# Writing out the order of every engine beside the products of a blocked attention and gated-unit kernel

## The chip, the cores and the metric

The kernel runs on one core of a Trainium2 chip. The metric is the device time of the whole kernel in microseconds (us). TensorE (PE) multiplies matrices into PSUM, VectorE (DVE), ScalarE (ACT) and GpSimd (POOL) work element by element, and SyncE (SP) issues most DMAs. Each engine works through its own instructions in the order in which they were put out, and waits for others by semaphores.

## The reference

Eight batches of 576 positions with eight heads of 64 go through attention, and the 4608 resulting rows of 512 through a gated unit with an inner width of 1536. Four heads see the last 32 positions, four see every 32nd position.

```python
B, H, S, D = q.shape
scores = scale * np.matmul(q, k.transpose(0, 1, 3, 2))
mask_local = (rel >= 0) & (rel < stride)
mask_strided = (rel >= 0) & (pos[None, :] % stride == pos[:, None] % stride)
scores = np.where(masks[None, :, :, :], scores, -1000000000.0)
...
attn = np.exp(scores)
attn = attn / (np.sum(attn, axis=-1, keepdims=True) + 1e-09)
...
gate = 1.0 / (1.0 + np.exp(-(x @ w_gate)))
val = x @ w_val
return (gate * val @ w_out).astype(np.float32)
```

## The kernel before

**Arithmetic.** Every float32 operand of the gated unit is split into a high part, which TensorE's fp32r format holds, and the low rest. A product is three matmuls: high x high, high x low, low x high (`three`, L407 to L409; `outs`, L437 to L442). All of them are of 128 x 128 weights by 512 columns.

**Stages.** The first phase computes the attention of batches 0, 1 and 2 (512 of their 576 positions are a "chunk"; the 64 others are kept for the end), brings in the weights, and computes the gated unit of batch 0 directly. Then come four superblocks of two chunks each: batches 1 and 2, 3 and 4, 5 and 6, and in the last batch 7 and the rests of all eight. A superblock multiplies two chunks with the two matrices of the gate and the value (g and v) in 2 x 2 blocks by seven products, P1 to P7, instead of eight. It does so in 6 pairs of weight blocks, 14 products a pair (P1 of g, P1 of v, P5 of g and so on), and then has 8 groups of output products, four for each chunk. The weights' mixtures that the seven products need are formed once, in superblock 1 (`load_mix`: sums and low parts on GpSimd, high parts on ScalarE), stored in DRAM, and loaded by the later superblocks.

**Beside a pair.** TensorE accumulates into six banks, called g1, g2, g5 and v1, v2, v5. `pair_of_chunks` copies (ACT) P1, P5 and P6 out of their banks, takes sigmoids (ACT, L539), adds (DVE, L537) and multiplies (DVE, L538, into `h`). A bank can be written again when its reader is done. `load_outs` splits `h` into high and low parts (L579, L580) for the output products. `store` copies the four sums of a chunk out of PSUM, ScalarE the first and third, VectorE the second and fourth, into the buffers of `OBS` (L458), and SP sends them out (L452).

**Attention beside it.** During a superblock, the attention of the next superblock's two batches runs in four steps per batch (`pair`): score matmuls (L189), mask, maximum and subtraction (`soft`, L203 to L209), exponential (ACT, L213), sum and division (`norm`, L217 to L220), eight 32x32 block transposes on VectorE (`turn_blocks`, L242), weighing matmuls (L270), copies to `raw` (`split_high`, L301). Batches 0 to 2 use TensorE's transposes (L228) and ScalarE's copies (L250) in place of VectorE's. When the eight steps are done, `mix_input` forms the seven mixtures of the next chunks (T: subtractions on VectorE, L342; h: high parts on ScalarE, L352; l: low parts on VectorE, L354).

**What sets the order.** In the first phase, `ORDER` is a list written out by hand; each word puts out one step on all engines. `Wf.i` loads weight f (i is 0 for the gate, 1 for the value, 2 for the output), `a`, `b`, `w`, `u`, `l` decode and split it, `g` is a product, `s`, `m`, `x`, `y` are the gate, `O` the output product; `Qbp`, `Sbp`, `Fbp` and so on are the attention step p of batch b, `J` a mixing input. In the superblocks only TensorE's order is written by hand (L646). The others' is chosen by a planner, which estimates when each instruction could start; the code raises the priority of the gate's and the output's instructions (`tc.high_priority`). The score of a step is put out every 12 products (24 with a single batch), its weighing 9.5 later, and the step's VectorE work is handed to the planner as a whole.

## Time and profile before

| | before |
|---|---|
| time, three runs | 1068.7 us median (1064.05 to 1069.07) |
| time of the profiled run | 1066.27 us |
| its span, first to last instruction | 1064.1 us |
| granted TensorE clock, mean | 0.953 |
| busy: PE, DVE, ACT, POOL | 953.2, 561.8, 447.6, 150.3 us |
| first product on a mixture | 204.4 us |
| last output product ends | 1056.3 us |

Rows of a timeline have the start, the length, the engine, the line and operation, and what is written from what; in brackets is the idle time before it on that engine and what ended it. Rows of waits have the total in us, how often, and the longest. Windows give each engine's busy time in a stretch. The granted clock is the share of full speed at which TensorE was let run. TensorE's row in a window can be full while its clock is low.

### The profile page before, as it was taken

To read this page: it belongs to the slowest core of one execution; us is meant where nothing else is said; L and a number is where in the kernel's file an instruction comes from. 1 tells how busy PE (TensorE), PEld (TensorE's weight loads), DVE (VectorE), ACT (ScalarE), POOL (GpSimd) and SP (SyncE) were. 2 spreads that over 40 slices of the span, in tenths; PEclk is the share of its full clock that TensorE was granted. 3 is DMA by queue.
4 is the path that set the end of the run, shared out by engine and by line. 5 is a ranking of instruction groups with operands and counts; after the bars stand their busy time and mean duration, and the time that the engine had idled before them with its cause. 6 is when DMAs were issued, how large, how long until landed. Compare 5 with 4: busy or idle time off the path is not lost.

```text
span 1064.1 us, 17875 instructions
## 1 busy us (share of the span) xinstructions
PE 953.2 (90%) x7576; PEld 763.5 (72%) x7576; DVE 561.8 (53%) x854; ACT 447.6 (42%) x782; POOL 150.3 (14%) x140
## 2 busy tenths in 40 slices
PE   4789977698989999799998996999989979999997
PEld 3577765577867887587776885878768858888885
DVE  5868865676768752366657833254466302323321
ACT  4677884456645430244445420344344203233221
POOL 1532476335740000000000000000000000000000
PEclk9999987699999999799989998999999989999998
DMA  7776776425652467465623778354315683362463
GB/s 273 251 253 209 235 247 254 158 108 197 254 212 108 169 241 272 179 225 195 272 88 119 252 249 345 123 222 186 154 65 187 241 331 155 139 236 100 165 231 99
DMA packets 38494, 212.80 MB, mean 200 GB/s; under 512 B 8080, under 2 KB 9232, under 8 KB 28176
## 3 DMA queue, kind: packets, MB, share of 16 engines
q1 hardware_dynamic: 35824, 201.55, 51.4%
q10 hardware_dynamic: 2592, 10.12, 2.8%
q8 instruction: 59, 0.97, 0.4%
q14 instruction: 19, 0.16, 0.0%
HBM read 172.86 MB, written 38.80 MB: 199 GB/s over the span
## 4 chain that ended last, share of the span: by engine, by line
PE 61%; DVE 13%; ACT 8%; DMA 8%; issue 7%; POOL 3%; SPq 0%; ACTq 0%; DVEq 0%; POOLq 0%
PE o L409 24%; PE o L442 13%; PE g L409 7%; PE v L409 6%; DVE pt L242 3%; PE g L442 3%; PE v L442 3%; PE x L270 3%; DMA out<-ob 2%; ACT L213 2%; PE s L189 2%; DMA wo<-outer 2%; DMA first_x1l<-in_w_all 1%; POOL mix L500 1%; POOL w L401 1%
## 5 line engine op out<-in xcount | busy, mean ns | idle before, releaser
L442 PE MATMUL o<-wo,hs 128*128 128x512 f32 x864 | 206.5, 390 | 2.1 <-DVE h L538 1.3
L442 PEld LDWEIGHTS o<-wo,hs 128*128 128x128 f32 x864 | 161.3, 188 | 37.9 <-DVE h L538 2.6
L538 DVE TENSOR_TENSOR h<-s,o 128x512 f32<-128x512 f32 x48 | 32.9, 685 | 142.6 <-PE o L409 137.2
L409 PE MATMUL o<-x0h,mix 128*128 128x512 f32 x192 | 74.8, 447 | 36.6 <-ACT ob L450 13.6
L580 DVE TENSOR_TENSOR hs<-h,hs 128x512 fp32r<-128x512 f32 x96 | 61.4, 686 | 84.7 <-ACT hs L579 82.8
L579 ACT CAST hs<-h 128x512 fp32r<-128x512 f32 x96 | 53.2, 620 | 94.6 <-PE o L442 50.7
L242 DVE STREAM_TRANSPOSE pt<-sb 32x320 f32<-32x320 f32 (+1 forms) x160 | 85.7, 536 | 2.6
L409 PE MATMUL o<-x,mix 128*128 128x512 f32 x288 | 76.0, 413 | 12.2 <-DVE h L538 8.0
L539 ACT ACTIVATE s<-s 128x512 f32<-128x512 f32 x48 | 30.3, 632 | 113.1 <-DVE s L537 113.1
L409 PEld LDWEIGHTS o<-x0h,mix 128*128 128x128 f32 x192 | 40.7, 212 | 51.8 <-ACT ob L450 14.3
L409 PEld LDWEIGHTS o<-x,mix 128*128 128x128 f32 x288 | 55.5, 196 | 27.5 <-DVE h L538 9.7
L170 POOL MEMSET sb<- 128x120 f32 x10 | 2.0, 199 | 462.2 <-DVE pt L242 462.2
L409 PE MATMUL o<-x2h,mix 128*128 128x512 f32 x192 | 64.2, 395 | 2.2 <-ACT gq L553 2.2
L409 PE MATMUL o<-x6h,mix 128*128 128x512 f32 x192 | 63.8, 393 | 0.0
L409 PE MATMUL o<-x3h,mix 128*128 128x512 f32 x192 | 63.5, 392 | 0.0
L551 ACT COPY o<-o 128x512 f32<-128x512 f32 x48 | 27.3, 571 | 74.5 <-PE o L409 74.3
L448 DVE COPY ob<-o 128x512 f32<-128x512 f32 x12 | 8.3, 692 | 73.9 <-PE o L442 58.9
L539 ACT ACTIVATE s<-o 128x512 f32<-128x512 f32 x48 | 28.8, 600 | 42.2 <-PE o L409 42.0
L409 PEld LDWEIGHTS o<-x2h,mix 128*128 128x128 f32 x192 | 36.0, 188 | 11.3 <-ACT gq L553 3.5
L401 POOL TENSOR_TENSOR w<-whole,w 128x512 fp32r<-128x512 f32 x24 | 34.6, 1453 | 54.3 <-ACT w L397 40.2
L409 PE MATMUL o<-x0l,mix 128*128 128x512 f32 x96 | 41.8, 435 | 0.0
L409 PEld LDWEIGHTS o<-x6h,mix 128*128 128x128 f32 x192 | 36.0, 188 | 8.0 <-DVE v L537 0.4
(160 smaller groups left out, 1892.6 us busy)
## 6 DMA issues: line engine op xcount, KB each, us to landing
mix<-mix SPq DMA_DIRECT2D x48, 1792.0 KB, 7.7
wo<-outer SPq DMA_DIRECT2D x32, 1536.0 KB, 6.6
first_x1h<-in_w_all SPq DMA_DIRECT2D x18, 512.0 KB, 4.9
first_x1l<-in_w_all SPq DMA_DIRECT2D x18, 512.0 KB, 5.0
out<-ob SPq DMA_DIRECT2D x32, 256.0 KB, 5.4
qk<-in_qk_l SPq DMA_DIRECT2D x12, 592.0 KB, 4.4
vv<-in_v_l SPq DMA_DIRECT2D x11, 640.0 KB, 5.9
outer<-w SPq DMA_DIRECT2D x12, 512.0 KB, 3.8
```

Of the source, the lines that this page charges most:

```text
L189: nc.tensor.matmul(sc[g * m : (g + 1) * m, j * BANK + s * kk : j * BANK + (s + 1) * kk], qk[d, q0 : q0 + m], qk[d, k0 : k0 + kk], start=Tr ...
L213: nc.scalar.activation(prob, prob, AF.Exp, scale=SCALE)
L242: nc.vector.transpose(dst[to : to + LB, :, col : col + LB], src[rows : rows + LB, :, h * LB : (h + 1) * LB])
L270: nc.tensor.matmul(xp[j * D : (j + 1) * D, r * BANK + (u * per + g) * m : r * BANK + (u * per + g + 1) * m], v[rows, (u * per + g) * P + j ...
L401: nc.gpsimd.tensor_tensor(l, words.pop((f, i))[0].bitcast(F32), h.bitcast(F32), op=ALU.subtract)
L409: nc.tensor.matmul(o, w, x, start=first and n == 0, stop=last and n == len(todo) - 1, skip_group_check=onto)
L442: nc.tensor.matmul(o, a[:, i * P : (i + 1) * P], b, start=first and n == 0, stop=last and n == 2)
L538: mul = lambda to, x, y: nc.vector.tensor_tensor(to, x, y, op=ALU.mult)
L539: sig = lambda to, x: nc.scalar.activation(to, x, AF.Sigmoid)
L551: run("P1", g1, v1, lambda: nc.scalar.copy(g2, g1), lambda: nc.scalar.copy(v2, v1))
L579: nc.scalar.copy(hh, src)
L580: nc.vector.tensor_tensor(hl, src, hh.bitcast(F32), op=ALU.subtract)
```

## The change

All engines' order is now written out, in the superblocks too. Each of the 132 products of a superblock (14 per pair, then the halves of the output products) is a place t. `before[t]` is put out ahead of it, `beside[t]` behind it, and behind that its own copies and gate operations. A step of attention has its score and mask at place 0, maximum, subtraction and exponential at 1, 2 and 3, the sum at 5, the division at 6, its eight transposes one each at 7 to 14, and its weighing at 16, which is place 2 of the next step. Mixtures are formed at the places of `FORM`, and loaded in two DMAs, the first three slots ahead (`W_OF` has a new order of slots).

The strided steps of batches 3 to 7 get a second buffer for their probabilities (`sb2`, `mx2`). Output copies go to eight buffers, t0 to t3 for a superblock's first batch and t4 to t7 for its second, which the pairs use for temporary results. The output sums use other banks: g5, v5, g1, v1 for the first chunk, g2, v2, g5, v5 for the second.

`ORDER` is a new list. Of the 36 `u` (high parts of weights) 17 become `U`, on GpSimd; of the 12 `y` (low parts of the gate's result) seven become `Y`, on GpSimd; two of the seven `Jl` become `JL`, on GpSimd. `M0..` and `M1..` form the first two mixtures in place of the planner. `e` is the store of batch 0. Attention steps come earlier in the list. One row of it before and one after:

```diff
-E22 u11.2 N22 T21 l11.2 P21 m11 X20 Jh2 Z23 x11 Jl2 V22 H20 y11 R20 S23 O11 F23 T22 E23 P22 N23 X21 H21 V23 R21 X22
+E23 u11.2 M0k H22 M1ls u11.2 JT1 R22 l11.2 x11 Jh1 T23 y11 Jh2 O11 JL1 P23
```

The rest of the diff, cut to what the text speaks of:

```diff
 SECOND = (4, 5)
 GROUPS = 2 * NF // THREE
-PIECE_0, PIECE, PIECE_X = 1, 12, 9.5
 SUPER = ((1, 2), (3, 4), (5, 6), (7, None))
-W_OF = dict(P1=0, P2=1, P4=2, P5=3, P6=4, P7=5, P3=6)
+W_OF = dict(P1=0, P5=1, P6=2, P2=3, P7=4, P3=5, P4=6)
...
@@ -150,6 +150,8 @@
         def part(tag, n):
             if not second:
+                if tag in ("sb", "mx") and b >= BY_PE and not local:
+                    return flat(tag + "2", n, f"{tag}{b}_{step}")
                 return flat(tag, n, f"{tag}{b}_{step}")
...
+        def most():
+            prob, row, by_row = rows()
             nc.vector.tensor_reduce(row, prob, axis=AX.X, op=ALU.max)
+        def less():
+            prob, row, by_row = rows()
             nc.vector.tensor_tensor(prob, prob, by_row, op=ALU.subtract)
+        def soft():
+            mask(), most(), less()
...
-        def norm():
+        def total():
             prob, row, by_row = rows()
             nc.vector.tensor_reduce(row, prob, axis=AX.X, op=ALU.add)
+        def share():
+            prob, row, by_row = rows()
             nc.vector.tensor_scalar_add(row, row, 1e-9)
             nc.vector.reciprocal(row, row)
             nc.vector.tensor_tensor(prob, prob, by_row, op=ALU.mult)
+        def norm():
+            total(), share()
...
+        def turn_block(m):
+            if m == 0:
+                tiles["pt"] = part("pt", 2 * SS * QB)
+            src, dst = (tiles[x][:, : 2 * ns * QB].rearrange("p (t k) -> p t k", k=QB) for x in ("sb", "pt"))
+            n, h = divmod(m, 2)
+            to, rows, col = (n // 2 * 2 + h) * LB, n * LB, n % 2 * LB
+            nc.vector.transpose(dst[to : to + LB, :, col : col + LB], src[rows : rows + LB, :, h * LB : (h + 1) * LB])
...
-            nc.vector.tensor_tensor(xs[m][1], src, xs[m][0].bitcast(F32), op=ALU.subtract)
+            engine.tensor_tensor(xs[m][1], src, xs[m][0].bitcast(F32), op=ALU.subtract)
...
+    def upper(f, i, copy=nc.scalar.copy):
+        copy(parts_of(f, i)[1], words[f, i][0].bitcast(F32))
...
-    OBS = ("ob0", "ob1", "ob0", "ob1")
+    OBS = tuple(("t0", "t1", "t2", "t3", "t4", "t5", "t6", "t7")[n : n + NTT] for n in (0, NTT))
...
-        if f == NF - 1:
-            store(acc.pop(0), 0, OBS)
...
+    EARLY = 3
     def load_mix(s, p, i):
-        t = next_of_ring(f"mix{s + 1}_{p}_{i}", 2 * MIX)
-        hold["mix", i, p] = t
-        if s:
-            nc.sync.dma_start(t.bitcast(F32), mixed[p, i])
-            return
+        t = hold["mix", i, p] = next_of_ring(f"mix{s + 1}_{p}_{i}", 2 * MIX)
+        cut = EARLY * 2 * PART
+        for lo, hi in ((0, cut), (cut, 2 * MIX)):
+            nc.sync.dma_start(t[:, lo:hi].bitcast(F32), mixed[p, i][:, lo:hi])
...
+        def rest_of(which):
+            src, at = srcs[which]
+            to = mix_parts(t[0])[:, at]
+            tt(to[:, :, 1], src(), to[:, :, 0].bitcast(F32), op=ALU.subtract)
...
     def group_of_outs(s, n, banks, tick):
         j, g = divmod(n, GROUPS // 2)
         (g1, g2, g5), (v1, v2, v5) = banks
-        accs = ([g1, v1, g5, v5], [g1, v1, g2, v2])[j]
-        h, w = hold["h"].pop(0), hold["o"].pop(0)
+        accs = ([g5, v5, g1, v1], [g2, v2, g5, v5])[j]
+        h, w = hold.pop(("h", n)), hold.pop(("o", n))
         for q in range(THREE):
             f = g * THREE + q
             cut = [slice((2 * q + k) * TB, (2 * q + k + 1) * TB) for k in range(2)]
-            tick(2)
-            outs(accs, [h[:, c] for c in cut], [w[:, c] for c in cut], f == 0, f == NF - 1)
+            for k in range(2):
+                with tick():
+                    half = slice(k * NTT // 2, (k + 1) * NTT // 2)
+                    outs(accs[half], [h[:, c] for c in cut], [w[:, c] for c in cut], f == 0, f == NF - 1, half.start)
         if g == GROUPS // 2 - 1:
-            b = SUPER[s][j]
-            last = s == len(SUPER) - 1 and j
-            with tc.high_priority():
-                store(accs, b, ("ob0", "ob1", "t0", "t1") if last else OBS)
+            store(accs, SUPER[s][j], OBS[j])
...
+        elif kind == "e":
+            store(acc[0], 0, OBS[0], [int(of)])
...
+    FORM = ((0, "+"), (0, "ca"), (1, "cd"), (2, "la"), (2, "ld"), (3, "cs"), (3, "ct"), (4, "ls"), (4, "lt"), (5, "k"))
+    FORM_AT = (0, 6)
+    STEP = ((1, "F1"), (2, "F2"), (3, "E"), (5, "N0"), (6, "N1"))
+    TURN_AT = (7, 8, 9, 10, 11, 12, 13, 14)
+    TURN_LATE = (7, 7, 8, 8, 9, 9, 10, 10)
+    WEIGH, WEIGH_LATE = 16, 12
+    ONE = 2 * PARTS
+    FIRST = PAIRS * ONE
+    ALL = FIRST + 2 * 2 * NF
...
+        for p in range(PAIRS - 1):
+            for i in range(2):
+                if s:
+                    put(p * ONE, load_mix, s, p + 1, i)
+                else:
+                    f = form_mix(p + 1, i)
+                    for t, what in FORM:
+                        at = p * ONE + FORM_AT[i] + t
...
+        for n in range(GROUPS):
+            at = FIRST + (n - 1) * 2 * THREE if n else FIRST - ONE
+            put(at, load_outs, s, n)
+            for q in range(THREE):
+                put(at + (2 * q if n else 4 * q + 1), split_outs, s, n, q)
+        if not last:
+            for i in range(2):
+                put(ALL - 2 * THREE, load_mix, s + 1, 0, i)
...
+            of = [b for b in SUPER[s + 1] if b is not None]
+            steps = [(b, p, pairs[b, p]) for b in of for p in range(4)]
+            for q, (b, p, do) in enumerate(steps):
+                at = q * ONE
+                late = q == len(steps) - 1
+                put(at, do["Z"], where=before)
+                put(at, lambda do=do, b=b, p=p: do["S"](bank("a", f"s{b}_{p}")), where=before)
+                put(at, do["F0"])
+                if not late:
+                    put(at, steps[q + 1][2]["Q"])
+                elif s + 2 < len(SUPER):
+                    put(at, steps_later["Q"])
+                for t, what in STEP:
+                    put(at + t, do[what])
+                for n, t in enumerate(TURN_LATE if at >= FIRST else TURN_AT):
+                    put(at + t, do["B"], n)
+                x = at + (WEIGH_LATE if late and at >= FIRST else WEIGH)
+                put(x, lambda do=do, b=b, p=p: do["X"](bank("a", f"x{b}_{p}")), where=before)
+                put(x, do["H"])
+                put(x, do["R"])
+                if not late:
+                    put(x, steps[q + 1][2]["V"])
+                elif s + 2 < len(SUPER):
+                    put(x, steps_later["V"])
+            for n, what in enumerate(MIX_INPUTS):
+                put(at + n * 2 // 3, mix_input, s + 1, what)
...
+        @contextmanager
+        def tick():
+            for do, args in before[clock[0]]:
+                do(*args)
+            yield
+            for do, args in beside[clock[0]]:
+                do(*args)
+            clock[0] += 1
...
     with tc.manual_schedule():
         for what in ORDER.split():
             step(what)
-
-    with tc.manual_schedule(engines={mybir.EngineType.PE}):
-        stages = []
         for s in range(len(SUPER)):
-            stages += [(s, "p", p) for p in range(PAIRS)] + [(s, "o", n) for n in range(GROUPS)]
-
-        def load(s, kind, n):
-            if kind == "p":
-                load_mix(s, n, 0), load_mix(s, n, 1)
...
-                    gap = PIECE * 2 // len(of)
-                    todo = [t for q in range(len(of) * 4) for t in (PIECE_0 + q * gap, PIECE_0 + q * gap + PIECE_X)]
-                    todo.append(max(todo[-1], PAIRS * 2 * PARTS + 2))
...
-            if k + 1 < len(stages):
-                load(*stages[k + 1])
-            (pair_of_chunks if kind == "p" else group_of_outs)(s, n, banks, tick)
+            superblock(s)
```

VectorE in superblock 2, pair 3, before (the names: `pt` and `sb` are the transposed and the plain probabilities of an attention step, `s`, `v`, `gp`, `gq`, `vp`, `vq` temporary results of the gate, `o`, `g`, `v` the banks, `h` the result):

```order
L537 TENSOR_TENSOR v_2_3_4906<-o_1_4034,vp_3_4762 128x512
L220 TENSOR_TENSOR sb_0_4816<-sb_0_4816,mx_0_4817 128x640
L538 TENSOR_TENSOR h_7_4733<-s_2_3_4897,v_2_3_4906 128x512
L537 TENSOR_TENSOR s_2_3_4915<-g_4035,gq_3_4800 128x512
L242 STREAM_TRANSPOSE pt_0_4867<-sb_0_4816 32x10x32 x8
L537 TENSOR_TENSOR v_2_3_4924<-v_4036,vq_3_4808 128x512
L538 TENSOR_TENSOR h_7_4733<-s_2_3_4933,o_1_4034 128x512
L538 TENSOR_TENSOR h_6_4732<-s_2_3_4915,v_2_3_4924 128x512
```

and now:

```order
L258 STREAM_TRANSPOSE pt_3_4818<-sb_3_4671 32x12x32
L567 TENSOR_TENSOR v_2_3_4838<-o_1_4061,vp_3_4782 128x512
L258 STREAM_TRANSPOSE pt_3_4818<-sb_3_4671 32x12x32
L567 TENSOR_TENSOR s_2_3_4847<-g_4062,gq_3_4790 128x512
L568 TENSOR_TENSOR h_7_4670<-s_2_3_4828,v_2_3_4838 128x512
L258 STREAM_TRANSPOSE pt_3_4818<-sb_3_4671 32x12x32
L567 TENSOR_TENSOR v_2_3_4858<-v_4063,vq_3_4799 128x512
L258 STREAM_TRANSPOSE pt_3_4818<-sb_3_4671 32x12x32
L568 TENSOR_TENSOR h_6_4669<-s_2_3_4847,v_2_3_4858 128x512
L258 STREAM_TRANSPOSE pt_3_4818<-sb_3_4671 32x12x32
L568 TENSOR_TENSOR h_7_4670<-s_2_3_4867,o_1_4061 128x512
```

The eight transposes stood in one piece ahead of the last gate operations of the pair. They now stand singly between them.

VectorE at the border between superblocks 1 and 2, before (`ob` are output buffers, `cst` the mask, `mx` maxima and sums):

```order
L448 COPY ob_1_4024<-o_1_2064 128x512
L203 TENSOR_TENSOR sb_0_4049<-s_0_4051,cst 128x640
L208 TENSOR_REDUCE mx_0_4050<-sb_0_4049 128x10
L209 TENSOR_TENSOR sb_0_4049<-sb_0_4049,mx_0_4050 128x640
L217 TENSOR_REDUCE mx_0_4050<-sb_0_4049 128x10
L218 TENSOR_SCALAR mx_0_4050<-mx_0_4050 128x10
L219 RECIPROCAL mx_0_4050<-mx_0_4050 128x10
L220 TENSOR_TENSOR sb_0_4049<-sb_0_4049,mx_0_4050 128x640
L242 STREAM_TRANSPOSE pt_0_4100<-sb_0_4049 32x10x32 x8
L448 COPY ob_3_4030<-o_1_2064 128x512
```

and now (`hs` is the split result, which the last output group reads):

```order
L611 TENSOR_TENSOR hs_7_3961<-h_11_3223,hs_7_3961 128x512
L455 COPY ob_1_4051<-o_1_2069 128x512
L455 COPY ob_3_4057<-v_2071 128x512
L205 TENSOR_TENSOR sb_0_4068<-s_0_4070,cst 128x640
L213 TENSOR_REDUCE mx_0_4069<-sb_0_4068 128x10
L217 TENSOR_TENSOR sb_0_4068<-sb_0_4068,mx_0_4069 128x640
L228 TENSOR_REDUCE mx_0_4069<-sb_0_4068 128x10
L232 TENSOR_SCALAR mx_0_4069<-mx_0_4069 128x10
L233 RECIPROCAL mx_0_4069<-mx_0_4069 128x10
L234 TENSOR_TENSOR sb_0_4068<-sb_0_4068,mx_0_4069 128x640
L258 STREAM_TRANSPOSE pt_0_4187<-sb_0_4068 32x10x32
```

The second output copy stood behind a whole step of attention. Both copies now stand ahead of it.

TensorE at the end of the first phase, from behind its last gate and value product, before (`t` transposes, `x` weighing, `s` scores, `o` the output sums; the numbers behind `t`, `x` and `s` are the attention step):

```order
L228 MATMUL t_1_1776<-cst,first_x_103 128x128 x6
L270 MATMUL x_0_1788<-pt_0_1629,vv_0_1612 64x32 x36
L189 MATMUL s_3_1836<-first_x_103 64x54 x24
L442 MATMUL o_0_666<-w_1659,first_x6l 128x512 x6
L442 MATMUL o_1_667<-w_1659,first_x6l 128x512 x6
L228 MATMUL t_2_1889<-cst,sb_2_1657 128x128 x4
L232 MATMUL t_2_1889<-cst,sb_2_1657 64x64 x2
L270 MATMUL x_1_1904<-first_x_104 64x54 x22
L270 MATMUL x_2_1934<-pt_2_1897,vv_2_1831 64x32 x36
L228 MATMUL t_3_1974<-cst,first_x_103 128x128 x6
L270 MATMUL x_3_1987<-first_x_104 64x54 x22
L189 MATMUL s_0_2103<-qk_0_2095 32x64 x40
```

and now, from the last gate and value product on:

```order
L416 MATMUL v_11_1933<-xh_3_91,w_1833 128x512
L449 MATMUL o_0_837<-w_1719,first_x2l 128x512 x6
L449 MATMUL o_1_838<-w_1719,first_x2l 128x512 x6
L245 MATMUL t_3_1979<-cst,first_x_103 128x128 x6
L449 MATMUL o_0_837<-w_1833,first_x6l 128x512 x6
L449 MATMUL o_1_838<-w_1833,first_x6l 128x512 x6
L286 MATMUL x_3_2006<-first_x_104 64x54 x22
L191 MATMUL s_0_2078<-qk_0_1594 32x64 x40
```

Before, three transposes, one score and four weighings of batch 2 stood there, and batch 3's first score. Now one transpose, one weighing and that score are left.

More of the change, by code (lines that the diff above doesn't have):

```diff
@@ L1 @@
-from contextlib import ExitStack
+from contextlib import ExitStack, contextmanager
 import numpy as np
@@ L319, in bank @@
         return ps.tile([P, 2 * BANK], F32, tag=tag, name=name)
[L321 to L330 removed]
     xs = {}
     def mix_input(s, what):
+        engine = nc.gpsimd if what[0] == "L" else nc.vector
+        what = what.lower() if what[0] == "L" else what
         a, b = (raw[n] for n in SUPER[s])
@@ L541, in run, with sum_of @@
         def run(which, g, v, after_g, after_v, first=True):
-            steps = both(which, g, v, first)
-            next(steps)
-            with tc.high_priority():
-                after_g()
-            next(steps)
-            with tc.high_priority():
-                after_v()
-            next(steps, None)
+            for o, m, after in ((g, gm, after_g), (v, vm, after_v)):
+                with tick():
+                    product(o, m, which, first)
+                after()
+        def sum_of(n, o, which):
+            add(new("s" + n), o, tmp["g" + which])
+            sig(tmp["s" + n], tmp["s" + n])
         run("P1", g1, v1, lambda: nc.scalar.copy(g2, g1), lambda: nc.scalar.copy(v2, v1))
```

248 lines of the change are left out of this document (130 added, 118 removed).

## Prediction

> **What bounds the kernel now.** I read the windows first, cut where the work changes. The first products of superblocks 1 to 4 start at 204.4, 428.3, 656.5 and 869.4 us, and TensorE's last product ends at 1056.3. The columns are the stretch, its length and each engine's busy us with its number of instructions; then the granted clock, the DMA share and GB/s.
>
> ```profile
> core 0: us, PE busy (x) PEld busy (x) DVE busy (x) ACT busy (x) POOL busy (x), PEclk, DMA share, GB/s
> 0.00:204.40 204.40, 155.10 (x2049) 122.17 (x2049) 140.51 (x202) 132.00 (x248) 90.51 (x78) 0.92 0.70 242
> 204.40:428.30 223.90, 208.51 (x1771) 166.38 (x1768) 144.43 (x219) 103.90 (x177) 58.56 (x56) 0.96 0.52 193
> 428.30:656.50 228.20, 209.99 (x1768) 167.36 (x1768) 130.94 (x211) 87.84 (x150) 0.80 (x4) 0.95 0.55 204
> 656.50:869.40 212.90, 196.09 (x1200) 157.55 (x1200) 94.91 (x146) 72.91 (x122) 0.40 (x2) 0.96 0.50 190
> 869.40:1056.30 186.90, 183.48 (x792) 150.09 (x792) 49.69 (x75) 50.49 (x88) 0.00 (x0) 0.98 0.45 172
> 1056.30:1064.10 7.80, 0.00 (x0) 0.00 (x0) 1.29 (x2) 0.47 (x1) 0.00 (x0) 0.66 0.59 134
> ```
>
> In the superblocks TensorE is the bound: 93% busy in the first, 98% in the fourth, with the other engines far below. The fourth has no attention beside it. How fast TensorE can go is read from a stretch of the chain that ended last (start, length, what), and from its score (line 189) and weighing (line 270) matmuls over superblocks 1 to 3, one row each.
>
> ```profile
> 389.16 16.32 PE o L442 x72
> ```
>
> ```profile
> 204.40:869.40 665.00, 18.57 (x1203) 0.96 0.53 196
> ```
>
> ```profile
> 204.40:869.40 665.00, 24.52 (x1160) 0.96 0.53 196
> ```
>
> One 128x512 matmul takes 16.32 / 72 = 0.2267 us when nothing is in its way. A superblock has 6 pairs x 14 products x 6 + 8 groups x 36 = 792 of them, so 179.5 us, and the four have 718. Attention adds 18.6 + 24.5 = 43 us, and I add 4 us for its 40 hand-overs between small and large matmuls. The floor of the four superblocks is thus 765 us. They take 1056.3 - 204.4 = 851.9. The excess is 87 us.
>
> The waits of TensorE (us in total, times, longest) name it:
>
> ```profile
> PE o L409 <- ACT ob L450: 13.6, 3, 5.2
> PE o L409 <- DVE h L538: 13.6, 7, 2.7
> PE o L409 <- DVE ob L448: 11.9, 3, 4.8
> PE o L409 <- ACT s L539: 9.8, 6, 2.0
> ```
>
> Two kinds: output copies at the three borders between superblocks (25.5 us), and gate work inside them (23.4 us). What is left of the 87 us is mostly the lower clock behind them. The border between superblocks 1 and 2 in order of time:
>
> ```profile
> 427.67 0.59 ACT L450 COPY ob<-o 128x512 f32<-128x512 f32 x1 [5.55 <-DMA out<-ob]
> 428.31 0.79 PE L409 MATMUL o<-x0h,mix 128*128 128x512 f32 x1 [5.21 <-ACT ob L450]
> 431.10 4.12 DVE L242 STREAM_TRANSPOSE pt<-sb 32x320 f32<-32x320 f32 x8
> 435.25 0.69 DVE L448 COPY ob<-o 128x512 f32<-128x512 f32 x1
> 435.99 0.80 PE L409 MATMUL o<-x0h,mix 128*128 128x512 f32 x1 [4.76 <-DVE ob L448]
> ```
>
> ```profile
> 430.00:444.00 14.00, 9.24 (x28) 6.84 (x28) 5.74 (x11) 2.32 (x4) 0.20 (x1) 0.61 0.52 211
> ```
>
> ScalarE's second copy waits 5.55 us for the DMA that empties the first of two buffers. TensorE, whose next product writes the bank that is being copied, waits 5.21 us. Then VectorE's second copy stands behind eight transposes of the next batch, and TensorE waits 4.76 us more. After that the clock is 0.61. A border therefore costs 10 us of waiting and some 5 us of slow products. Inside a superblock:
>
> ```profile
> 523.43 4.10 DVE L242 STREAM_TRANSPOSE pt<-sb 32x320 f32<-32x320 f32 x8
> 527.56 0.69 DVE L537 TENSOR_TENSOR v<-v,vq 128x512 f32<-128x512 f32 x1
> 528.76 0.68 DVE L538 TENSOR_TENSOR h<-s,v 128x512 f32<-128x512 f32 x1
> 528.90 0.50 PE L409 MATMUL o<-x0h,mix 128*128 128x512 f32 x1 [1.86 <-DVE h L538]
> ```
>
> Again a block of eight transposes, 4.1 us, stands ahead of the gate products, and the next pair's first product waits for the bank that they read.
>
> **The change, part by part.** *Order inside the pairs.* Work beside product t is now put out at product t, one transpose at a time, so at most one transpose (4.10 / 8 = 0.51 us) and one addition stand ahead of what a bank waits for. A bank is written again four products after its reader is due, 4 x 1.36 = 5.4 us. VectorE's work per pair with attention is about 8 us of softmax and transposes and 8 x 0.69 = 5.5 us of gate work, 13.5 of some 21.4 us. A measured stretch agrees:
>
> ```profile
> 441.10:482.10 41.00, 39.24 (x395) 31.27 (x393) 22.47 (x36) 20.27 (x33) 0.00 (x0) 1.00 0.45 162
> ```
>
> VectorE is busy 22.5 of 41 us, ScalarE 20.3. At two products VectorE gets 1.9 us of work for 1.36 us and runs 1 us late, under the 5.4 us that it may be. So I take the 23.4 us and their slow clock as gone, with 1 us a superblock kept.
>
> The second set of probabilities lets the mask of the next step start before the last transpose of the present one; without it VectorE would be held at products 14 and 15 only. I cost it at nothing.
>
> *Borders.* Outputs get four buffers for each batch, and the second batch's accumulators are now other banks than the next superblock's first two products write. The four copies need 2 x 0.59 us on ScalarE and 2 x 0.69 us on VectorE, while products 0 and 1 (2.7 us) run on free banks. What is late next: buffers 4 to 7 are also those of the sigmoids, the first of them at product 6, 9.5 us after the border. The copies end at about 1 us, and a store lands in 5.4 us by the median row below. If one took 8 us more than that, a sigmoid would wait; I keep 0. The mixtures of the next superblock are issued 8.2 us before the border and land in 7.7 us each:
>
> ```profile
> mix<-mix SPq DMA_DIRECT2D x48, 1792.0 KB, 7.7
> out<-ob SPq DMA_DIRECT2D x32, 256.0 KB, 5.4
> ```
>
> The first three of seven slots now come in a DMA of their own, which covers products 0 to 5. I cost the additional issues on SP at nothing, since SP has 8 us of cover; without it a border would cost up to 3 us.
>
> *The first superblock* forms the mixtures of five pairs on GpSimd at fixed products, where the old planner had begun some of them earlier. VectorE also starts it late: of the mixing inputs, three subtractions and three splittings follow the last batch's weighing, about 7 us by the row below, and the first mask stands behind them. I keep 4 us of waits for the first pair.
>
> ```profile
> L342 DVE TENSOR_TENSOR raw<-raw 128x1024 f32<-128x1024 f32 x7 | 8.6, 1223 | 2.4 <-ACT raw L301 2.3
> ```
>
> *The first phase.* Cut at 140 us the windows show where it goes wrong, and the chain shows the longest piece in it:
>
> ```profile
> 20.00:140.00 120.00, 104.87 (x1175) 81.74 (x1173) 92.61 (x141) 91.21 (x168) 47.79 (x39) 1.00 0.72 239
> 140.00:160.00 20.00, 14.57 (x170) 11.18 (x163) 14.96 (x17) 15.38 (x31) 17.93 (x13) 0.85 0.74 259
> 160.00:180.00 20.00, 15.53 (x242) 12.44 (x242) 12.02 (x14) 9.64 (x17) 16.10 (x15) 0.76 0.67 249
> 180.00:200.00 20.00, 9.42 (x138) 7.44 (x137) 9.10 (x12) 7.78 (x19) 8.28 (x7) 0.67 0.67 250
> 200.00:204.40 4.40, 2.89 (x125) 2.58 (x125) 1.62 (x2) 2.25 (x8) 0.00 (x0) 0.50 0.13 43
> ```
>
> ```profile
> 192.29 8.00 DMA first_x<-in_v_s
> ```
>
> Up to 140 us TensorE is 87% busy. After that the last batch's attention is alone on the path, step behind step, with a wait of 8.00 us for its values. At full clock the work after 140 us is 14.57 x 0.85 + 15.53 x 0.76 + 9.42 x 0.67 + 2.89 x 0.50 = 32 us. The new order has only one transpose and one weighing left after the last gate products. At the earlier density the 32 us take 32 / 0.874 = 36.5, and 3 us are left for the end of the last step: 180 us. Bounds: 172 (no wait after 140) and 204.4 (nothing gained); I take 180, since only the tail's order is at fault.
>
> For this GpSimd gets 17 castings from ScalarE, and seven splittings and two of 1024 columns from VectorE. Its casting isn't in the trace; the bounds are ScalarE's row and GpSimd's two-input row:
>
> ```profile
> L401 POOL TENSOR_TENSOR w<-whole,w 128x512 fp32r<-128x512 f32 x24 | 34.6, 1453 | 54.3 <-ACT w L397 40.2 <-issue 14.1
> L397 ACT CAST w<-whole 128x512 fp32r<-128x512 f32 x24 | 15.0, 624 | 1.1 <-DVE whole L387 1.0
> ```
>
> That is 17 x 0.62 to 1.45, plus 7 x 1.45, plus 2 x 2.9 (twice the columns), so 26 to 41 us on top of 90.5: at most 131 of 180 us. I take 1.0 for a casting, between the two. With GpSimd so far under its bound the moved work is off the path, and it relieves ScalarE and VectorE of 11 and 8 us. The GPSIMD Engine Reference of the Trainium skill speaks against the move: its "Engine selection" would leave two-input elementwise work to VectorE, as about twice as slow on GpSimd. The trace bears that out (1453 ns against VectorE's 690 for 512 columns); the sum stays the same by it, since the work is off the path.
>
> **The sum.** Time and span of the profiled run are 1066.3 and 1064.1, so 2.2 us lie around it; that run is 2.4 us under the median of 1068.7. First phase 180; superblocks 765 + 4 + 4 = 773; tail 7.8, unchanged; 2.2: **963 us**. Against the profiled run that is 24 us from the first phase and 79 from the superblocks.
>
> **Rivals.** *The first phase isn't shortened:* 204.4 in place of 180 gives 987. For it: all engines are between 65% and 77% busy there, and a wait can move. Against: the loss sits in 60 of 204 us. *New waits in the pairs:* every engine now waits in program order, and half of the removed excess comes back: 963 + 40 = 1003. For it: no row shows this order. Against: the 5.4 us of room. *GpSimd becomes the first phase's bound,* because its operations stretch while VectorE works beside them: at 1.56 times as long its 131 us are 204, so about 987. For it: it has the most added work. Against: the 1453 ns were taken with VectorE 69% busy (140.51 of 204.4 us) already, so the stretch would have to come from the little that is added. That the two engines share their SBUF interfaces and contend is stated in the Trainium skill (GPSIMD Engine Reference, "Specifications"); no row here separates the two.
>
> *Slower:* ScalarE's exponential at product 3 waits for mask, maximum and subtraction, and two copies behind it free the bank of product 8. These rows price it:
>
> ```profile
> 514.60 0.84 DVE sb L203
> 517.22 1.28 ACT L213
> 518.51 0.75 ACT sb L213
> ```
>
> Product 8 starts 13.2 us after the pair; table, exponential and two copies take 1.28 + 0.75 + 2 x 0.59 = 3.2. So it decides from 10 us on, and by 0.84 us an operation VectorE is done at 4. If it were done only at 15.5, each of the 20 steps of attention would lose 5.5 us: 963 + 110 = 1073.
>
> **Chances.** Forecast (946 to 980) 0.68; first phase as before 0.13; new waits 0.10; GpSimd 0.04; slower 0.03; 0.02 for losses that cancel the gain to within 0.5%, about what a measurement here can tell from no change. So faster 0.95, same 0.02, slower 0.03. The range goes from 946 (172, no waits) to 1004, which takes in the first phase unchanged and most of the new waits.
>
> **What would show it.** Right: the first product on a mixture near 180 us; no wait for an output copy at any border; clock 1.00 across it; superblocks of about 204, 200, 191 and 180 us; single transposes between gate operations. Wrong: waits of TensorE for h, s or gq over 10 us in total, GpSimd over 90% busy before 180 us, or a superblock over 210 us.

## The result, and the profile after

| | before | after |
|---|---|---|
| time, median of runs side by side | 1066.4 us (4 runs, 1061.1 to 1069.1) | 976.3 us (4 runs, 975.1 to 978.2) |
| ratio, 95% interval | | 0.916 (0.912 to 0.921) |
| profiled run, its span | 1066.3, 1064.1 us | 978.2, 976.3 us |
| granted clock, mean | 0.953 | 0.982 |

The kernel is 8.4% faster. The forecast of 963 us was 13 us too low, and the time lies inside its range, 946 to 1004.

The windows of the kernel after, cut at the first product of each superblock and at the end of the last product (columns as in the prediction):

```profile
0.00:183.64 183.64, 156.27 (x2049) 122.96 (x2049) 141.72 (x194) 117.68 (x226) 95.83 (x88) 0.92 0.68 234
183.64:397.42 213.78, 205.92 (x1772) 162.61 (x1769) 149.63 (x216) 106.28 (x191) 87.42 (x86) 0.99 0.58 222
397.42:600.24 202.82, 201.27 (x1774) 161.38 (x1769) 133.78 (x211) 84.37 (x147) 0.80 (x4) 1.00 0.60 228
600.24:789.75 189.51, 189.51 (x1207) 154.17 (x1201) 97.74 (x148) 72.50 (x122) 0.20 (x1) 1.00 0.57 216
789.75:969.80 180.05, 180.05 (x793) 148.31 (x791) 50.30 (x76) 51.23 (x89) 0.00 (x0) 1.00 0.50 190
```

The first phase went from 204.4 to 183.6 us, the superblocks from 223.9, 228.2, 212.9 and 186.9 to 213.8, 202.8, 189.5 and 180.1: 20.8 us from the first phase and 65.7 from the superblocks. The rest of the difference of the spans is the tail, 7.8 to 6.5. In superblocks 2 to 4 TensorE is now busy for 570.8 of 572.4 us at a clock of 1.00. What it still waits for from 183.64 us on (total us, times, longest):

```profile
PE o L416 <- ACT gq L583: 3.5, 5, 0.9
PE o L416 <- ACT o L581: 2.8, 1, 2.8
PE x L286 <- DVE sb L205: 2.1, 2, 1.1
PE o L449 <- DVE ob L455: 0.9, 2, 0.4
```

Against 48.9 us in the four rows of before, for output copies, `h` and `s`, this is little, and the first two rows lie in superblock 1 alone. The border between superblocks 1 and 2, in order of time:

```profile
395.13 3.56 SPq L459 DMA_DIRECT2D out<-ob  x4
395.88 0.59 ACT L457 COPY ob<-g 128x512 f32<-128x512 f32 x1 [0.77 <-PE g L449]
396.45 1.04 PE L191 MATMUL s<-qk 64*32 64x64 f32 x80
396.56 0.69 DVE L455 COPY ob<-v 128x512 f32<-128x512 f32 x1 [0.67 <-PE v L449]
397.42 0.50 PE L416 MATMUL o<-x0h,mix 128*128 128x512 f32 x1
```

No row of TensorE has a bracket: the copies follow their sums at once, SP issues four stores in 3.56 us, and the first product starts behind the score without a wait.

What is left of the loss is in superblock 1: 213.8 us against 202.8 in superblock 2, which has the same products. The first pair and the second show it, in this order:

```profile
183.38 3.38 POOL L361 TENSOR_TENSOR x<-raw,x 128x1024 fp32r<-128x1024 f32 x1 [4.17 <-ACT x L359]
184.50 3.34 DVE L361 TENSOR_TENSOR x<-raw,x 128x1024 fp32r<-128x1024 f32 x1
...
191.23 1.04 ACT L359 CAST x6h<-raw 128x1024 fp32r<-128x1024 f32 x1 [5.63 <-DVE raw L349]
193.34 0.79 PE L416 MATMUL o<-x3h,mix 128*128 128x512 f32 x1 [2.80 <-ACT o L581]
...
217.34 1.14 ACT L528 CAST mix<-sums 128x512 fp32r<-128x512 f32 x2
218.50 1.28 ACT L224 ACT_TABLE_LOAD   x1
219.80 0.75 ACT L224 ACTIVATE sb<-sb 128x648 f32<-128x648 f32 x1
220.92 0.58 ACT L583 COPY gq<-o 128x512 f32<-128x512 f32 x1
221.55 0.50 PE L416 MATMUL o<-x2h,mix 128*128 128x512 f32 x1 [0.65 <-ACT gq L583]
```

Above: VectorE's mixing inputs take long beside GpSimd's, ScalarE stands idle for 5.63 us at the cast that needs the last of them, and the copy of product 0, behind that cast in ScalarE's order, lets TensorE wait 2.80 us. Below: at product 3 of each pair two mixture casts stand ahead of table load, exponential and copies, so `gq` ends late. The product that waits reads x2h, so it is P2 of g, product 6. It writes bank g1, while `gq` is read from g2. The two banks are the halves of one tile. That was the first sign I noticed that a reader has less room than I had counted.

### The profile page after: what moved, and what is told of

Same layout as the page of the kernel before. It is cut to its first block, busy times and chain, and to the rows that moved or that the text cites. A ratio compares the mean times of both kernels' runs of the same rounds, so it can differ in the third digit from the quotient of the medians.

```text
span 976.3 us, 18003 instructions
## 1 busy us (share of the span) xinstructions
PE 933.0 (96%) x7576; PEld 749.4 (77%) x7576; DVE 573.9 (59%) x845; ACT 432.1 (44%) x773; POOL 184.2 (19%) x178
## 4 chain that ended last, share of the span: by engine, by line
PE 74%; DVE 10%; ACT 6%; DMA 4%; POOL 4%; issue 2%; SPq 0%; ACTq 0%; DVEq 0%; POOLq 0%
PE o L416 30%; PE o L449 12%; PE g L416 8%; PE g L449 6%; PE v L449 6%; PE v L416 6%; PE x L286 3%; PE s L191 2%; DMA first_x1h<-in_w_all 2%; POOL w L408 2%; DMA first_x1l<-in_w_all 1%; DVE pt L258 1%; POOL mix L533 1%; ACT L224 1%; DVE sb L234 1%
## 5 line engine op out<-in xcount | busy, mean ns | idle before, releaser
L449 PE MATMUL o<-wo,hs 128*128 128x512 f32 x576 | 148.3, 392 | 0.9 <-DVE ob L455 0.9
L449 PEld LDWEIGHTS o<-wo,hs 128*128 128x128 f32 x576 | 107.2, 188 | 26.7 <-DVE ob L455 2.3
L449 PE MATMUL g<-wo,hs 128*128 128x512 f32 x288 | 81.9, 393 | 0.0
L449 PE MATMUL v<-wo,hs 128*128 128x512 f32 x288 | 81.0, 389 | 0.0
L416 PE MATMUL o<-x,mix 128*128 128x512 f32 x288 | 71.9, 398 | 0.0
L416 PE MATMUL o<-x0h,mix 128*128 128x512 f32 x192 | 66.3, 406 | 0.0
L449 PEld LDWEIGHTS v<-wo,hs 128*128 128x128 f32 x288 | 54.1, 188 | 11.4
L449 PEld LDWEIGHTS g<-wo,hs 128*128 128x128 f32 x288 | 53.4, 188 | 11.2
L228 DVE TENSOR_REDUCE mx<-sb 128x10 f32<-128x640 f32 (+1 forms) x26 | 21.3, 820 | 63.5 <-ACT sb L224 63.5
L416 PEld LDWEIGHTS o<-x3h,mix 128*128 128x128 f32 x192 | 36.7, 191 | 10.9 <-ACT o L581 3.2
```

The costliest lines, as they stand in the source:

```text
L228: nc.vector.tensor_reduce(row, prob, axis=AX.X, op=ALU.add)
L416: nc.tensor.matmul(o, w, x, start=first and n == 0, stop=last and n == len(todo) - 1, skip_group_check=onto)
L449: nc.tensor.matmul(o, a[:, i * P : (i + 1) * P], b, start=first and n == 0, stop=last and n == 2)
```

## The experiments

Theory: three parts shorten the kernel, each by itself: single transposes between the gate operations, eight output buffers, and the first phase's order. The further loss in superblock 1 is ScalarE's order. Rivals stand with each run. All kernels are the kernel after with the edit that is shown, and times are to be read against its 976.3 us and ratio 0.916.

### Transposes in one block, at product 7 or at 12

```
-    TURN_AT = (7, 8, 9, 10, 11, 12, 13, 14)
-    TURN_LATE = (7, 7, 8, 8, 9, 9, 10, 10)
+    TURN_AT = (7,) * 8
+    TURN_LATE = (7,) * 8
```

The other kernel has `(12,) * 8` and `(10,) * 8` there.

> All eight transposes of a step are put out in one block at product 7. Theory now (TensorE waits for the last reader of the pair of banks that lie in one tile, so a reader due at product t is waited for at t + 2, with one product, 1.36 us, between): the block of 4.1 us holds the product h1 at 7, product 9 waits 0.7 to 1 us for it in each of 20 steps, so +15 to +20: 990 to 996, with waits for h at the products of kind X5 or behind them. Rival (the prediction's own room of four products, 5.4 us): no wait, 976 within 2. Second rival (any block costs what blocks cost before the change): +38 or more.

> All eight transposes in one block at product 12 (10 in the last late step), about where a block stood before the change. Theory (room of one product between): the block runs from about product 12 on, the last gate product h2 ends 2.8 us late, and the next pair's second product, which writes that tile, waits 1 to 1.5 us a step: +20 to +30, so 996 to 1006, and the waits for h come back as before the change. Rival (room of 5.4 us): no wait, 976 within 3.

Measured: 1022.8 us, ratio 0.960 (0.957 to 0.963), and 1014.7 us, 0.952 (0.949 to 0.956): 46 and 38 us slower than single transposes. TensorE's waits for `h` are back, for the blocks at 7 and at 12 (one row of each kernel):

```profile
PE o L416 <- DVE h L568: 31.3, 14, 4.1
```

```profile
PE o L416 <- DVE h L568: 21.6, 14, 2.6
```

One step with the block at 7, in order of time:

```profile
448.83 4.65 DVE L258 STREAM_TRANSPOSE pt<-sb 32x384 f32<-32x384 f32 x8
...
453.51 0.69 DVE L568 TENSOR_TENSOR h<-s,o 128x512 f32<-128x512 f32 x1
454.26 1.05 PE L416 MATMUL o<-x,mix 128*128 128x512 f32 x2 [2.07 <-DVE h L568]
```

The multiplication that reads v1 ends at 454.20; product 9, which writes v2, the other half of the same tile, starts at 454.26. So a reader due at product t is waited for at t + 2, and the room of 5.4 us falls: the rival with no wait is out by 38 us and more. The mechanism of the theory holds, but not its size, which reached what the second rival gave: a wait is 31.3 / 14 = 2.2 us in the mean with the block at 7 and 1.5 at 12, where 0.7 to 1 and 1 to 1.5 were expected, and the clock falls behind some of them (0.93 in the pair from 437.9 to 463.9 us). That the wait follows the tile and not the bank is read from such rows, in this kernel and in others, and from the code; a kernel with the banks as separate tiles was not tried.

### Two output buffers

```
-    OBS = tuple(("t0", "t1", "t2", "t3", "t4", "t5", "t6", "t7")[n : n + NTT] for n in (0, NTT))
+    OBS = (("t6", "t7", "t6", "t7"),) * 2
```

> Outputs go through two buffers again (those of two sums that are first written at product 8), the new banks for the second batch stay. Theory (the buffers, waiting for the stores, made the borders expensive): copies 3 and 4 wait 2 to 5 us for the first stores, TensorE's product 2 or 3, which writes their banks, waits 1.5 to 4 us at each of three borders, with slow clock behind: 5 to 18 us, so 982 to 994. Rival (the free banks were enough, since two products cover the copies): under 2 us in all, 976 to 978.

Measured: 1002.8 us, ratio 0.940 (0.933 to 0.948), 26 us slower. The cause is the theory's, but the loss is larger than the 5 to 18 us that it gave. A border in order of time:

```profile
402.06 8.78 SPq L459 DMA_DIRECT2D out<-ob  x4
408.19 0.59 ACT L457 COPY ob<-g 128x512 f32<-128x512 f32 x1 [6.15 <-DMA out<-ob]
408.83 0.50 PE L416 MATMUL g<-x1h,mix 128*128 128x512 f32 x1 [1.42 <-ACT ob L457]
410.93 1.35 SPq L496 DMA_DIRECT2D mix<-mix  x3
```

ScalarE waits 6.15 us for a store to leave its buffer, with the copy of product 0 queued behind. SP needs 8.78 us to put out four stores, and the loads of the next mixtures stand behind them on its queue. By windows, superblocks 1 to 4 take 220.1, 208.7, 192.9 and 187.2 us, so 3 to 7 us more each. TensorE also waits for such copies in the output products, between a superblock's two batches (6.8 us, 4 times), which I had not counted.

### The banks of before, with eight buffers

```
-        accs = ([g5, v5, g1, v1], [g2, v2, g5, v5])[j]
+        accs = ([g1, v1, g5, v5], [g1, v1, g2, v2])[j]
```

> Eight output buffers stay, but the accumulators of both batches are those of before, so that the next superblock's first two products write banks that are still being copied. Theory (with buffers free the copies end 0.6 and 1.3 us after the last product): waits of 1 to 2 us at each of three borders, two of the copies on one tile with the next product; +3 to +8 with the clock behind, 979 to 984. Rival (the banks and not the buffers made the borders expensive): +8 us a border, 1000.

Measured: 980.3 us, ratio 0.920 (0.913 to 0.926). That lies in the theory's range and can't be told from 0.916 either, so the profile has to say. Superblocks 2 to 4 take 203.0, 190.4 and 180.9 us, 1.9 more than after in all, and the border between superblocks 1 and 2 has no wait:

```profile
393.64 1.04 PE L191 MATMUL s<-qk 64*32 64x64 f32 x80
393.74 1.29 DVE L455 COPY ob<-o 128x512 f32<-128x512 f32 x2 [7.25 <-PE o L449]
394.60 0.50 PE L416 MATMUL o<-x0h,mix 128*128 128x512 f32 x1
```

The score matmuls, 1.04 us, cover the copies. Of the expected waits of 1 to 2 us a border, one of 0.5 us is there, at the last border, and the rival's 8 us are not. What the old banks do cost lies elsewhere: in each superblock TensorE waits once for `h` in the output products, 3.1 us in all. The row at 526.22 us in superblock 2 is the start of the second sum, which is written to v1 just behind the multiplication that reads v2. At the borders it is the buffers that count.

### One set of probabilities

```
-                if tag in ("sb", "mx") and b >= BY_PE and not local:
-                    return flat(tag + "2", n, f"{tag}{b}_{step}")
```

> Only the second set of probabilities is taken away: all steps use one. Theory (the prediction costed it at nothing: the next step's memset and mask are then held by the last transpose or weighing at products 14 and 15 only): under 2 us in all, 975 to 979. Rival (the weighing of a step at product 16 comes two products after the next step's mask, and without the second set the mask, maximum and exponential follow late, and the copies behind them): 0.5 to 1 us in each of 20 steps, 986 to 996.

Measured: 975.5 us, ratio 0.918 (0.913 to 0.922): no difference. The second set costs and brings nothing that these runs can tell, as forecast.

### No work moved to GpSimd

```
-S02 b0.1 U0.0 P01 w0.1 X00 l0.0 W1.1 F02 u0.1 Z03 H00 l0.1 S03 V02 a1.0 b1.0 L00 E02 F03 g0.1.0 R00 g0.0.0 a1.1 W0.2
+S02 b0.1 u0.0 P01 w0.1 X00 l0.0 W1.1 F02 u0.1 Z03 H00 l0.1 S03 V02 a1.0 b1.0 L00 E02 F03 g0.1.0 R00 g0.0.0 a1.1 W0.2
```

So with every `U`, `Y` and `JL` of the list (both rows are cut at the same words).

> The new order of the first phase stays, but its 17 castings go back from GpSimd to ScalarE, and the seven splittings and two of 1024 columns back to VectorE, at the same places. Theory (the order alone shortens the first phase, and the moved work was off the path): first phase of 180 to 188 us where it is 178 to 184 now, the time at 974 to 984. Rival (the relief of ScalarE and VectorE made the gain): first phase of 195 to 204 us, the time at 988 to 998.

Measured: 976.4 us, ratio 0.916 (0.910 to 0.921), first phase 184.5 us. The moved work brings nothing. The first phase's windows without it, to be set against the first of the five windows of the kernel after:

```profile
0.00:184.50 184.50, 151.81 (x2049) 118.76 (x2049) 137.34 (x202) 126.44 (x243) 74.68 (x66) 0.95 0.68 233
```

The kernel after spares VectorE eight instructions, 202 to 194, and yet VectorE is busy longer with it, 141.7 us against 137.3.

### GpSimd and VectorE side by side

```
+        for n in range(4):
+            sub(nc.vector, d2, d0, d1)
...
+        for n in range(4):
+            sub(nc.gpsimd, p2, p0, p1)
...
+        for n in range(8):
+            sub(nc.vector, d2, d0, d1)
+            sub(nc.gpsimd, p2, p0, p1)
...
+        for n in range(8):
+            sub(nc.vector, d2, pa, d1)
+            sub(nc.gpsimd, p2, p0, p1)
```

> The kernel as changed, and behind it, on data of no use, subtractions of 128x1024 float32: four on VectorE alone, four on GpSimd alone, then both at once with all operands in SBUF, then both with VectorE reading one operand from PSUM, then GpSimd's subtractions beside VectorE's copies. Theory (the two engines hold each other up where VectorE reads two operands from SBUF): alone 1.2 and 2.4 to 2.8 us, at once both over 3, and with a PSUM operand VectorE back at 1.2. Rival (the first pair's long VectorE operation had another reason, as the DMA traffic there): 1.2 and 2.8 in every block.

The time of this kernel is not compared, since the trial stands behind the last product. Its timeline (a row with x8 runs from the first's start to the last's end; `trial_h` is in SBUF, `trial_a` in PSUM):

```profile
969.39 4.94 DVE L806 TENSOR_TENSOR trial_h<-trial_h,trial_h 128x1024 f32<-128x1024 f32 x4
975.59 9.59 POOL L806 TENSOR_TENSOR trial_h<-trial_h,trial_h 128x1024 f32<-128x1024 f32 x4
985.95 22.87 DVE L806 TENSOR_TENSOR trial_h<-trial_h,trial_h 128x1024 f32<-128x1024 f32 x8
988.15 25.29 POOL L806 TENSOR_TENSOR trial_h<-trial_h,trial_h 128x1024 f32<-128x1024 f32 x8
1014.73 10.03 DVE L806 TENSOR_TENSOR trial_h<-trial_a,trial_h 128x1024 f32<-128x1024 f32 x8
1015.87 19.30 POOL L806 TENSOR_TENSOR trial_h<-trial_h,trial_h 128x1024 f32<-128x1024 f32 x8
1036.46 18.61 DVE L829 COPY trial_h<-trial_h 128x1024 f32<-128x1024 f32 x8
1066.02 2.88 DVE L836 COPY trial_h<-trial_h 128x1024 f32<-128x1024 f32 x4
```

Alone VectorE takes 4.94 / 4 = 1.24 us and GpSimd 9.59 / 4 = 2.40. At once it is 22.87 / 8 = 2.86 and 25.29 / 8 = 3.16 (GpSimd's last two run alone). With one operand in PSUM VectorE takes 10.03 / 8 = 1.25 and GpSimd 19.30 / 8 = 2.41: as if alone. VectorE's copy goes from 2.88 / 4 = 0.72 to 18.61 / 8 = 2.33. The theory holds, though VectorE's 2.86 us stay just under the 3 that it gave, and the traffic as a cause is out for this size. The GPSIMD Engine Reference of the Trainium skill ("Specifications") names contention with VectorE's instructions that have two SBUF inputs or run in a two-port mode. The trial agrees for two inputs, and shows what it costs: each engine slower by 1.3 to 2.3 times. A copy with one input suffers too, which would have to be the page's two-port mode; the trace doesn't name modes.

### The first phase in its old order

The list of before takes the place of the new one; the words that form the first two mixtures (behind O8 and O9), store batch 0 and load batch 3's first inputs are put in. Three pieces of it:

```
... O8 M0+ M0ca M0ct M0la M0cs M0ls M0lt M0cd ...
... O9 M1+ M1ca M1ct M1lt M1cd M1ld M1la M0ld M1cs M0k M1ls M1k ...
... O11 e0 e3 e2 e1 ...
```

> The first phase in the order of before (with the first mixtures and output copies put behind the products that free their memory), the superblocks as they are. Theory (the order of the tail was at fault): the first product on a mixture comes at 200 to 208 us, the time at 993 to 1001, superblocks unchanged within 3 us. Rival (the first phase gains by something else, as the mixtures' forming): 180 to 190 us.

Measured: 1009.4 us, ratio 0.945 (0.940 to 0.951). The first product on a mixture comes at 216.2 us, 12 us later than in the kernel before and 8 us over the theory's upper end, and the time misses its 993 to 1001 as well, so this run doesn't price the order cleanly. Some of it is my placing of the mixtures, as one wait of TensorE shows:

```profile
160.81 1.22 PE L417 MATMUL v<-xh,w 128*128 128x512 f32 x2 [4.02 <-POOL w L409]
```

It is for GpSimd, which forms the mixtures ahead of that weight's split. The rival is out, though: what the new code has besides the order does not bring 180 to 190 us. With the run without GpSimd's work, the order is what is left for the 20.8 us, by elimination. The kernel after shows the gain where the prediction had looked for it, behind 140 us:

```profile
140.00:160.00 20.00, 18.84 (x159) 15.04 (x155) 16.95 (x21) 14.92 (x30) 13.22 (x12) 1.00 0.54 175
160.00:183.64 23.64, 19.55 (x305) 14.90 (x303) 19.90 (x22) 16.86 (x34) 19.38 (x15) 0.91 0.52 197
```

TensorE is busy there for 38.4 of 43.6 us, at a clock of 0.91 and more; in the prediction's three rows from 140 us on and the short one behind them it was 42.4 of 64.4, at 0.85 to 0.50. Its waits in that stretch add up to 21.9 us before and 5.3 us after.

The row of the new list that stands under "The change" lacks words. In the kernel it begins `E23 w11.2 M1la g11.1 Y10 s11 N23 M0ld M1cs O10 m11 M0k H22`.

### Superblock 1: later casts, a later last input, both

```
-    FORM = ((0, "+"), (0, "ca"), (1, "cd"), (2, "la"), (2, "ld"), (3, "cs"), (3, "ct"), (4, "ls"), (4, "lt"), (5, "k"))
+    FORM = ((0, "+"), (0, "ca"), (1, "cd"), (2, "la"), (2, "ld"), (5, "cs"), (5, "ct"), (6, "ls"), (6, "lt"), (7, "k"))
```

```
-Jl2 X23 e0 e3 e2 e1 M1k H23 R23 JT3 Jh4 JT2 Jh5 JL4 Jh3 Jl5 Jl3 JT4 V30 Jh6 Jl6
+Jl2 X23 e0 e3 e2 e1 M1k H23 R23 JT3 Jh4 JT2 Jh5 JL4 Jh3 Jl5 Jl3 V30
+        if s == 0:
+            put(7, mix_input, 0, "T4")
+            put(7, mix_input, 0, "h6")
+            put(8, mix_input, 0, "l6")
```

> Only the mixture casts cs and ct (and what follows them) are put two products later, behind the copies vp and gq. Theory (in superblock 1 ScalarE's two casts of 0.57 us at product 3, ahead of table load, exponential and the copies, make product 8 wait 0.65 us in each pair): the waits of TensorE for gq in superblock 1 fall from 3.5 us to under 0.5, pairs 2 to 6 go from 22.7 to about 21.7 us, and superblock 1 from 213.8 to about 209; 971 us in all. Rival (these pairs are long because GpSimd and the stores of the mixtures work beside them): pairs stay at 22.7 us and the time at 976.

> Only the last mixing input (one subtraction, cast and splitting of 1024 columns) is put out at products 7 and 8 of the first pair, not ahead of it. Theory (VectorE's subtraction for it, 3 us late beside GpSimd, holds ScalarE's cast and so the first product's copy, and TensorE's third kind of product waits 2.8 us for that; the half clock follows): that wait goes, the half clock at 193 to 196 us too, superblock 1 from 213.8 to 209; 971 us. Rival (the first mask, which is behind the same VectorE operations, is what ends last): the wait moves to the exponential or gq, and no more than 1 to 2 us are gained.

> Both edits: later mixture casts and later last mixing input. If the two losses are apart, the gains add: superblock 1 near 205 us and 967 in all. If they are one loss seen twice (the copies of the first pair), superblock 1 stays at 208 to 209 and the time at 971.

Measured: 975.7 us, ratio 0.917 (0.912 to 0.923); 975.3, 0.916 (0.911 to 0.921); 973.3, 0.915 (0.910 to 0.920). Superblock 1 takes 214.1, 213.0 and 211.3 us. None reached what its theory gave, and both edits together miss both of their forecasts. Each edit alone moved a wait. With later casts:

```profile
241.09 1.28 ACT L569 ACT_TABLE_LOAD   x1
242.38 0.60 ACT L569 ACTIVATE s<-o 128x512 f32<-128x512 f32 x1
243.03 3.02 PE L416 MATMUL o<-x,mix 128*128 128x512 f32 x12 [0.77 <-ACT s L569]
```

With a later last input:

```profile
194.07 0.80 PE L416 MATMUL o<-x2h,mix 128*128 128x512 f32 x1 [2.87 <-ACT gq L583]
```

My theory of the casts failed as I had put it: `gq` came in time, and the sigmoid of product 6, now with casts ahead of it, was late for product 8 in its place. The rival that GpSimd makes these pairs long fits the time as well; the next kernel tells the two apart. For the last input the rival came out, a wait moved from one copy to the next and 0.7 us gained in superblock 1.

### ScalarE's queue clear at products 3 to 7

```
-    FORM = ((0, "+"), (0, "ca"), (1, "cd"), (2, "la"), (2, "ld"), (3, "cs"), (3, "ct"), (4, "ls"), (4, "lt"), (5, "k"))
-    FORM_AT = (0, 6)
+    FORM = ((0, "+"), (0, "ca"), (1, "cd"), (2, "la"), (2, "ld"), (8, "cs"), (8, "ct"), (9, "ls"), (9, "lt"), (10, "k"))
+    FORM_V = ((9, "+"), (9, "ca"), (10, "cd"), (10, "la"), (10, "ld"), (13, "cs"), (13, "ct"), (13, "ls"), (13, "lt"), (14, "k"))
...
-Jl2 X23 e0 e3 e2 e1 M1k H23 R23 JT3 Jh4 JT2 Jh5 JL4 Jh3 Jl5 Jl3 JT4 V30 Jh6 Jl6
+Jl2 X23 e0 e3 e2 e1 M1k H23 R23 JT2 JT3 Jh3 Jl3 Jh5 Jh4 V30
+            for t, what in ((3, "l5"), (4, "l4"), (7, "T4"), (7, "h6"), (8, "l6")):
+                put(t, mix_input, 0, what)
```

> The mixture casts cs and ct at products 8 and 13, the second mixture begun at 9, so that ScalarE has only its copies and the sigmoid at products 3 to 7; and the first pair's inputs cut so that VectorE does only one splitting ahead of the first mask, all of them on VectorE. Theory (moving the casts by two products only moved the wait to the sigmoid at product 6, since its room too is one product): no wait for gq or the sigmoid in superblock 1, pairs 2 to 6 from 22.7 to 21.9, first pair from 27 to 22.5; superblock 1 near 205, 967 in all. Rival (the pairs are long because GpSimd or the stores slow the engines): pairs stay over 22.5.

Measured: 967.1 us (6 runs), ratio 0.907 (0.905 to 0.910), beside 0.916 (0.912 to 0.921) for the kernel after. Its window of superblock 1, and its waits from 181.6 us on:

```profile
181.60:386.30 204.70, 202.95 (x1775) 162.38 (x1769) 146.17 (x217) 107.93 (x192) 79.72 (x82) 0.99 0.62 232
```

```profile
PE x L286 <- DVE sb L205: 2.2, 2, 1.1
PE o L449 <- DVE ob L455: 0.9, 2, 0.4
PE o L416 <- DVE h L568: 0.2, 1, 0.2
```

Superblock 1 is 9.1 us shorter and within 2 us of superblock 2 (202.7), with the same casts on ScalarE and the same mixtures on GpSimd. One thing besides the order differs: the splitting `JL4` of a mixing input has gone from GpSimd to VectorE. Starts of its pairs are 181.6, 203.3, 225.7, 247.1, 269.0 and 290.4: 21.7, 22.4, 21.4, 21.9 and 21.4 us each, as the theory said. In the kernel after the first took 27.2 us and the next four 90.7 together, against 87.1 here. For pairs 2 to 5 the rival is out, since GpSimd and the stores still work beside them. In the first pair, which gives 5.5 of the 9.1 us, the order and the splitting taken from GpSimd were not tried apart. This is the fastest of all the kernels, and faster than the one under study.

## Why the prediction was right, and where it was not

- *The bound: right; the floor: some 7 us too low.* The matmul of 0.2267 us and the 792 of them to a superblock give 179.5; superblock 4 took 180.05. The floor was put at about 200 for superblock 2, and 202.8 was measured. The hand-overs between small and large matmuls, 4 us for 40, had no row behind them. Superblock 3, in which TensorE waits for nothing, is 9.5 us longer than superblock 4. Its scores and weighings are busy for 2.95 + 4.52 = 7.5 us of that, so 2.0 are left for eight hand-overs: 0.25 us each, by this difference, where 0.1 was taken.
- *Order inside the pairs: the gain was right, the reason for its safety wrong.* The step that fails is "a bank is written again four products after its reader is due, 4 x 1.36 = 5.4 us". For readers of g1, g2, v1 and v2 the room is one product, since two banks share a tile. The single transposes, 0.5 us each, fit into it; a block doesn't, and costs 38 to 46 us. That the 1 us by which the prediction saw VectorE late is also less than one product, 1.36 us, is luck. In superblocks 2 to 4 no gate operation is waited for. The profile of before had shown the room already. At 528.90 us it is not the pair's first product that waits but the second, P1 of v, which writes v1; and it waits for a row that the prediction did not print, the multiplication that reads v2:

```profile
525.52 0.39 PE L409 MATMUL o<-x0h,mix 128*128 128x512 f32 x1
528.17 0.68 DVE L538 TENSOR_TENSOR h<-s,o 128x512 f32<-128x512 f32 x1
```

  The first row is the start of the first product, and the second ends at 528.85 us. The two waits at the border in the prediction are of this kind too: products 0 and 1 write g1 and v1, and the copies that they wait for are those of the third and fourth sums, g2 and v2.
- *Borders: right.* No wait for an output copy stands at any, and the clock is 1.00 across them. The two buffers cost 26 us in this kernel. The new banks, to which the text gave a share, brought nothing that can be told in the time. They were not the free banks that it took them for: g2 and v2 lie in the tiles of g1 and v1, which products 0 and 1 write. Only, they are now the first two of the four sums, and their copies end at 395.11 and 395.89 us, ahead of product 0 at 397.42. The cover for a late store was counted too long as well: 9.5 less 1 less 5.4 us leaves 3.1, not 8. It did not matter, since a store now lands in 2.3 us in the median.
- *The first superblock: mis-sized.* It was put at 204 us with 4 us of first-pair waits and took 213.8, over the 210 that the prediction itself had named as a sign of being wrong. It is 11.0 us longer than superblock 2, 6.9 in the first pair and 4.1 in pairs 2 to 5. The step that was mis-sized is ScalarE's order: the casts that form mixtures, of which the prediction told only GpSimd's part, and the last mixing inputs behind VectorE's longer subtractions. With that order mended, and one splitting taken from GpSimd, it took 204.7.
- *The rival that ends slower* had the right mechanism and place, ScalarE's queue at product 3 with the copies behind it. It worked in superblock 1 at 0.7 us a pair (3.5 us in five). Its point of decision, VectorE's softmax 10 us late, was worked out from the false room and from product 8; the product that waits first is 6.
- *The first phase:* 183.6 against 180. The same instructions up to the first mixture took 178.1 to 184.3 us in the profiles of seven kernels (after, later casts, two buffers, old banks, both blocks, one set), so 180 can't be told from it. No further gain is owed to GpSimd: the bound never came into play (95.8 us busy of 183.6), and the relief that the text counted for VectorE didn't show. In the rival of a first phase that isn't shortened, "all engines are between 65% and 77% busy there" leaves out GpSimd, which was busy for 90.5 of 204.4 us, 44%.
- *Second set of probabilities, additional DMA issues: right at nothing.* The second set was tried alone; the split loads weren't, but TensorE waits for no mixture.
- *The sum:* 180 + 773 + 7.8 + 2.2 was forecast, 183.6 + 786.2 + 6.5 + 1.9 measured. The mechanism was right. Of the 13 us by which the superblocks were too low, 7 are superblock 1's own loss (11.0 us against 4), and about 7 are the hand-overs, which come to 10.8 us for all 40 by differences like the one above, with superblock 1's set equal to superblock 2's. The other terms cancel to under 1 us. The four lengths that the prediction names, 204, 200, 191 and 180, add up to 775, 2 more than its sum.

## What to carry to other kernels

When the order is written by hand, count for each reader of PSUM how many products lie until the next write to its tile, not to its bank, and keep every queue that holds such a reader free of anything else for that long. A wait that goes when one operation is moved may only change its name: look at the stage's length, not at the row that is gone. Work moved from VectorE to an idle GpSimd isn't free for VectorE if both work from SBUF.
